# Retention and a gated feed-forward block in one kernel: other places for the sums of the second weight's quarters, and for the last steps of block 1

## The chip, the cores and the metric

The kernel runs on one core of a Trainium2 chip. The time is the device time of one execution in microseconds (us), and a kernel is judged by the median of several executions. TensorE (PE) multiplies matrices, VectorE (DVE), ScalarE (ACT) and GpSimd (POOL) work elementwise, SyncE (SP) only issues transfers (DMAs). Each engine takes its instructions in its own order, and semaphores hold an instruction until what it needs is there.

## The reference

Inputs are q, k, v of shape (4 batches, 8 heads, 768 positions, 64), w_in (512 x 2048) and w_out (2048 x 512), random, the weights in float64 on the way in (the kernel narrows them itself).

```python
gamma = 1.0 - 2.0 ** (-5.0 - np.arange(H))
for t in range(S):
    state = gamma * state + einsum('bhd,bhe->bhde', k[:, :, t], v[:, :, t])
    y[:, :, t] = einsum('bhd,bhde->bhe', q[:, :, t], state) / sqrt(D)
x = y.transpose(0, 2, 1, 3).reshape(3072, 512)
h = x @ w_in
out = (h / (1 + exp(-1.702 * h))) @ w_out
```

## The kernel before

**Chunks and steps.** The retention is computed in 24 chunks of 64 positions (two batches at once, 12 chunks per pair of batches). `turn(j)` transposes chunk j's q and k (from chunk 8 on by VectorE, L251) and issues the loads of q and k for chunk j+2 on SP (L154: 8 loads each). `step(j, f)` runs four groups of small matmuls on PE: the scores of chunk j (L287), the state's update (L295), and the output of the chunk before, f, from the state (L304) and from its own scores (L310). The first two write the PSUM tile `pa`, the others `py`; there is one buffer of each. Behind them VectorE masks the scores (L316), adds to the state (L366), and writes the output into the tile `X` (L328, L345). A step also issues the loads of k and v of the next chunk on SP (L140), and POOL decays k (`decay`, L272) and the state (`aged`, L357).

**Blocks.** Four chunks of two batches fill a block of 512 tokens; there are six blocks. Each block has a first product (x by w_in), the gating on ScalarE, and a second product (g by w_out). From block 2 on, the first product (`up`, L469) multiplies by Strassen and Winograd's scheme: seven products of halves in place of eight, with sums of the operands prepared beforehand. `sums_x` (POOL, L440 to L443) makes the sums of `X` in slots 2, 4, 5 and 6. The second product of blocks 0 and 1 (`down`, L705) has seven such products in 28 units (n = 0 to 27), each unit 4 matmuls, which the profile shows as 8 passes. Its sums of g (`sums_g`, DVE L456 to L458 and POOL L459) are made beside the third product (units 8 to 11), for the fourth (units 12 to 15). A kept sum behind unit 19 (DVE, L712) and the four output tiles (`put`: DVE L681, output DMA on POOL L682) follow the units that complete them; the last output follows unit 27. From block 2 on the second product (`down49`, L572) applies the scheme twice, and so needs sums of quarters of w_out.

**The sums of w_out's quarters.** For each of the seven outer products, `inner_w2(i)` derives three of them in `X` slots 4 to 6 (three subtractions on DVE, L519), and SP writes them to a DRAM tile `W2D[i]` (L520, 768 KB). All seven calls use the same place in `X`, so each call's first subtraction waits until the transfer before has landed, and `sums_x` of block 1, which writes the same slots, waits for the seventh. Slots 4 to 6 of `X` also hold a part of block 0's g, whose last reader in block 0's second product is unit 19. `inner_w2_t3(i)` makes a fourth sum in place (DVE, L525) once block 1's products have read that part of w_out.

**Order.** PE's instructions stand in the order of the text. For the other engines a scheduler of the compiler takes the calls in the order of the text as a wish and places each instruction by when its operands are expected to be there; only what is pinned keeps its order. In block 1 the steps stand between the units of the second product: `between` is a list of calls, and one is taken off after every third unit, half of them empty:

```python
between = [lambda: (decay(2 * CB), load(2 * CB + 1, "v"))]
for j in range(2 * CB + 1, 3 * CB + 1):
    between += [lambda j=j: (step(j, j - 1), j < 3 * CB and turn(j + 1)), lambda: None]
between.pop()
```

With CB = 4, that puts the steps of chunks 9, 10, 11 and 12 after units 5, 11, 17 and 23, and `sums_x` is called right behind the last.

Of the kernel before, what the change touches and what calls it, by code (L numbers as in the profile page):

```python
# [28 lines left out]
def kernel(  # L29
# [38 lines left out]
    CB = 4  # L68
# [55 lines left out]
    def load(j, what="qkv"):  # L124

        b, c = j // NC * 2, j % NC
        rows = slice(c * D, (c + 1) * D)
        keep = tc.keep_in_program_order if j < 2 * CB else lambda i: i  # L130

        def plain(name, src, tag, bufs, engine=sp):
            t = two.tile([P, H, D], F32, name=name + "_in", tag=tag, bufs=bufs)
            QKV[name, j] = t
            for i in range(2):
                if j < 2 * CB:
                    keep(engine.dma_start(t[i * D:(i + 1) * D], src[b + i, :, rows, :].rearrange("h p d -> p h d")))
                else:
                    for r in range(2):
                        keep(engine.dma_start(t[r * D:(r + 1) * D, i * HP:(i + 1) * HP],  # L140
                                              src[b + i, r * HP:(r + 1) * HP, rows, :].rearrange("h p d -> p h d")))

        if j < 2 * CB:
            if "q" in what:
                plain("q", q, "q_sq", 2)
            if "k" in what:
                plain("kn", k, "k_sq", 2, sp if j else act)
        elif "q" in what:
            for name, src in (("q", q), ("k", k)):
                t = two.tile([P, H, D // C4, C4], F32, name=name + "_sq")  # L150
                for r0 in range(0, P, C4):
                    for n in range(D // C4):
                        t0 = c * D + n * C4
                        tc.keep_in_program_order(sp.dma_start(  # L154
                            t[r0:r0 + C4, :, n], src[b + r0 // D, :, t0:t0 + C4, r0 % D:r0 % D + C4]
                            .rearrange("h p d -> p h d")))
                QKV[name, j] = t
        if "v" in what:
            if j >= 2 * CB and c < NC - 1:
                plain("kn", k, "kn", 1)  # L160
            plain("v", v, "v", 2)
# [66 lines left out]
    def home(j, name):  # L228

        at = ["qT", "kT", "kd", "at"].index(name)  # L230
        shape = [[HP, P] if j < 2 * CB else [H, D]] * 2 + [[H, D], [2, HP, D]]
        shape = shape[at]
        if j >= 2 * CB:
            return one.tile([P] + shape, F32, name=name, tag=name, bufs=[2, 1, 1, 2][at])
        t = G[:, at, j % 2 * 2:j % 2 * 2 + 2].rearrange("p s t -> p (s t)")
        return t.rearrange("p (a b c) -> p a b c", a=2, b=HP) if at == 3 else t.rearrange("p (a b) -> p a b", a=shape[0])

    def turn(j):

        QT[j], KT[j] = home(j, "qT"), home(j, "kT")  # L240
        if j < 2 * CB:

            x = QKV.pop(("q", j)), QKV["kn", j]
            TURNED[j] = p = [ps.tile([P, HP, P], F32, name="pt", tag="y") for i in range(2)]
            for n in (1, 0) if j else (0, 1):
                for s in range(HP):
                    for r in range(2):
                        pe.matmul(p[n][HALF[r], s, :], x[n][:, HP * r + s, :], ident, start=True, stop=True)  # L248
        else:
            for t, name in ((QT[j], "q"), (KT[j], "k")):  # L250
                tc.keep_in_program_order(dve.transpose(  # L251
                    t.rearrange("p h t -> p (h t)"), QKV.pop((name, j)).rearrange("p h n d -> p (h n d)")))
        if 2 * CB <= j < NCH - 2:
            load(j + 2, "qk")
# [6 lines left out]
    def decay(j):  # L261

        if j % NC == NC - 1:
            return
        KD[j] = home(j, "kd")
        x = QKV["kn", j]
        if j < 2 * CB:

            for h in range(H):
                pin(act.activation(KD[j][:, h], x[:, h], AF.Copy, scale=cold[:, H + h:H + h + 1]))  # L270
        else:
            pool.tensor_mul(KD[j].rearrange("p (i s) d -> p i s d", i=2), x.rearrange("p (i s) d -> p i s d", i=2),  # L272
                            cold[:, None, H:H + HP, None].to_broadcast([P, 2, HP, D]))
# [40 lines left out]
    def masked(j):  # L314
        AT[j] = home(j, "at")
        pin(dve.tensor_mul(AT[j], PA.pop(j)[:, :, 0],  # L316
                           mask if j < 2 * CB else mask[:, 0:1].to_broadcast([P, 2, HP, D])))
# [42 lines left out]
    def updated(f):  # L360
        c = f % NC
        new, u = state[(c + 1) % 2], PU.pop(f)
        if c == 0:
            pin(dve.tensor_copy(new, u))
        elif c < NC - 1:
            pin(dve.tensor_add(new, new, u))  # L366

    def step(j, f=None):
        attend(j, f)
        if j is not None:  # L370
            masked(j)
            if j > 2 * CB:
                decay(j)
        if f is not None:
            c = f % NC
            if c == 0:
                updated(f)
            else:
                by_state(f)
            output(f)  # L380
            if 0 < c < NC - 1:
                aged(f)
                updated(f)
        if j is not None and 2 * CB < j < NCH - 1:
            load(j + 1, "v")
# [123 lines left out]
    def w2q(w):  # L509

        return [W2[:, w, u::2, e * P:(e + 1) * P] for u in range(2) for e in range(2)]

    def inner_w2(i):

        b11, b12, b21, b22 = w2q(ORDER[i][1])
        t = []
        for k, a in enumerate((b12, b22, b21)):
            t.append(X[:, 4 + k].rearrange("p c (d e) -> p (c d) e", e=P))
            dve.tensor_sub(t[k], a, t[k - 1] if k else b11)  # L519
        sp.dma_start(W2D[i].rearrange("p k d e -> p (k d e)"), X[:, 4:7].rearrange("p k c t -> p (k c t)"))  # L520

    def inner_w2_t3(i):

        b11, b12, b21, b22 = w2q(ORDER[i][1])
        dve.tensor_sub(b12, b22, b12)  # L525
# [291 lines left out]
    for name, i in [("0a", 0), ("0b", 1)] + [(str(p), 2 * p) for p in range(1, NFF)]:  # L817
        n = Narrow(i)
# [20 lines left out]
    for name in """  # L839
# [16 lines left out]
    """.split():  # L856
        works[name]()
    ordered[0] = False
    for m in range(NB):
        between = []  # L860
        if m == 0:
            between = [lambda: turn(2 * CB), lambda: step(2 * CB), lambda: None, lambda: None, lambda: turn(2 * CB + 1)]
        elif m == 1:
            between = [lambda: (decay(2 * CB), load(2 * CB + 1, "v"))]
            for j in range(2 * CB + 1, 3 * CB + 1):
                between += [lambda j=j: (step(j, j - 1), j < 3 * CB and turn(j + 1)), lambda: None]
            between.pop()
        elif 1 < m < NB - 1:
            last = min((m + 2) * CB, NCH - 1)
            for j in range((m + 1) * CB + 1, last + 1):  # L870
                between.append(lambda j=j: (step(j, j - 1), j < last and turn(j + 1)))
            if last == NCH - 1:
                between.append(lambda: step(None, NCH - 1))
        if m > 1:
            if m > 2:
                W1B[:] = [late.tile([P, 2, 7, 2, P], F32, name=f"W1B{i}", tag=f"late{i}") for i in range(2)]
                pool.dma_start(W1B[0], W1D[0])
            for d in range(NP // 2):
                up(d)
                if d == 0 and m > 2:  # L880
                    pool.dma_start(W1B[1], W1D[1])
                if d == 0 and m < NB - 1:
                    turn((m + 1) * CB + 1)
                if d == NP // 2 - 2:
                    ring = begin_ring()
                if m == 2:
                    for i in range(2 * d, min(7, 2 * d + 2)):
                        inner_w2_t3(i)
        for n, unit in enumerate(down(m) if m < 2 else down49(m, *ring)):
            unit()  # L890
            if m == 0 and n < NP and n % 2:
                sums_w2(n - 1)
            if m == 0 and NP <= n < 3 * NP // 2:
                sums_w2_t3(2 * (n - NP))
            if m == 1 and n % 8 == 3:
                sums_w1(n // 4)
            if m == 1 and n % 3 == 1 and n < 21:
                inner_w2(n // 3)
            if between and (n % 3 == 2 if m < 2 else n % 3 == 1):
                between.pop(0)()  # L900
                if m == 1 and not between:
                    sums_x()
            if 1 < m < NB - 1 and n == 11:
                sums_x()
# [46 lines left out]
```

## Time and profile before

| | |
|---|---|
| median of 3 runs | 679.7 us (677.56 to 680.57) |
| the profiled execution | 678.85 us, its span on the core 676.7 us |
| PE busy | 655.5 us, 97% of the span |
| VectorE, POOL, ScalarE busy | 437.0, 170.4 and 156.9 us |
| granted clock of TensorE | 0.995 |
| block 0's second product on PE | 160.98 to 211.05 us of the span |
| block 1's second product, with its steps | 211.05 to 273.40 us |
| block 2's first product begins | 273.40 us |

The span runs from the first to the last instruction; the rest of the execution's time lies around it. A group of rows named "L705 PE MATMUL pd<-W,G" is line 705 on TensorE, which writes the tile pd from W and G. The time in brackets behind a row of the timeline is how long its engine sat idle before it, with what it waited for. SPq is the queue on which SP issues its transfers.

### The profile page before, as it was taken

How to read it: one execution, taken by the hardware profiler on the slowest of the kernel's cores; microseconds unless marked ns; L12 is line 12 of the kernel's file. 1: busy time of each engine (PE TensorE's matmuls, PEld its weight loads, DVE VectorE, ACT ScalarE, POOL GpSimd, SP SyncE). 2: the span in 40 equal slices, each digit the busy share in tenths (PEclk: the TensorE clock that was granted, in tenths of full speed). 3: DMA queues.
4: the chain of work that ended last, by engine and by line, in shares of the span. 5: the costliest groups of instructions: out<-in, count | busy, mean ns of one | idle time of the engine just before them, and what ended most of it. 6: DMA issues, size and time to landing. Idle time of an engine off the chain costs nothing.

```text
span 676.7 us, 15331 instructions
## 1 busy us (share of the span) xinstructions
PE 655.5 (97%) x6502; PEld 568.5 (84%) x6502; DVE 437.0 (65%) x614; ACT 156.9 (23%) x313; POOL 170.4 (25%) x189
## 2 busy tenths in 40 slices
PE   7799999999999979899999999999999999999997
PEld 4788864747888868688999988999988999988997
DVE  3688880879856686155887255898154896254865
ACT  5665523321000000133200133200133200133210
POOL 3000000020279151300245700245800244500000
PEclk9899999999999999899999999999999999999999
DMA  9999732332314835422177572178572153502142
GB/s 183 214 218 226 193 125 79 132 91 45 68 63 198 289 76 140 110 32 94 48 175 172 137 231 99 49 174 179 124 238 98 52 154 111 220 29 94 47 156 94
DMA packets 143780, 88.97 MB, mean 131 GB/s; under 512 B 129472, under 2 KB 130752, under 8 KB 142688
## 3 DMA queue, kind: packets, MB, share of 16 engines
q1 hardware_dynamic: 134656, 48.33, 31.0%
q0 software_dynamic: 6752, 38.42, 15.8%
q10 hardware_dynamic: 2304, 1.25, 0.6%
q8 instruction: 51, 0.84, 0.5%
q14 instruction: 17, 0.14, 0.1%
HBM read 72.37 MB, written 15.47 MB: 130 GB/s over the span
## 4 chain that ended last, share of the span: by engine, by line
PE 81%; DMA 7%; SPq 5%; DVE 5%; issue 1%; POOL 1%; ACT 0%; POOLq 0%
PE pq L572 26%; PE px L469 16%; PE py L469 12%; PE ph L425 8%; PE ph L412 8%; DMA W2D<-X 4%; SPq L154 4%; PE pd L705 3%; DVE X L519 3%; PE pt L248 2%; PE pa L295 1%; PE pa L287 1%; PE py L310 1%; DMA v_in<-in_v_dram 1%; PE py L304 1%; SPq L140 1%
## 5 line engine op out<-in xcount | busy, mean ns | idle before, releaser
L572 PE MATMUL pq<-W,G 128*128 128x128 f32 x672 | 80.3, 276 | 0.0
L572 PEld LDWEIGHTS pq<-W,G 128*128 128x128 f32 x672 | 77.6, 192 | 0.6
L541 POOL DMA_DIRECT2D ring<-W2D x28 | 15.4, 552 | 231.6 <-PE px L469 121.2
L469 PE MATMUL px<-X,W1A 128*128 128x256 f32 x256 | 61.3, 386 | 3.1 <-POOL X L442 3.1
L469 PE MATMUL px<-X,W1B 128*128 128x256 f32 x256 | 59.8, 379 | 0.0
L572 PE MATMUL pq<-ring,own 128*128 128x128 f32 x448 | 59.8, 276 | 0.0
L469 PEld LDWEIGHTS px<-X,W1A 128*128 128x128 f32 x256 | 49.0, 193 | 10.3 <-POOL X L442 3.5
L705 PE MATMUL pd<-W,G 128*128 128x256 f32 x224 | 50.4, 382 | 4.7 <-DVE G L458 4.7
L572 PEld LDWEIGHTS pq<-ring,own 128*128 128x128 f32 x448 | 54.5, 192 | 0.4
L469 PEld LDWEIGHTS px<-X,W1B 128*128 128x128 f32 x256 | 48.6, 190 | 6.6
L705 PEld LDWEIGHTS pd<-W,G 128*128 128x128 f32 x224 | 42.0, 190 | 11.7 <-DVE G L458 3.9
L469 PE MATMUL py<-X,W1A 128*128 128x256 f32 x192 | 45.8, 381 | 0.0
L469 PE MATMUL py<-X,W1B 128*128 128x256 f32 x192 | 45.4, 379 | 0.0
L391 ACT ACTIVATE G<-G 128x512 f32<-128x512 f32 x48 | 30.2, 630 | 52.0 <-DVE G L479 33.4
L469 PEld LDWEIGHTS py<-X,W1A 128*128 128x128 f32 x192 | 36.9, 192 | 5.2
L469 PEld LDWEIGHTS py<-X,W1B 128*128 128x128 f32 x192 | 36.5, 190 | 5.0
L487 DVE TENSOR_TENSOR t<-py,u 128x512 f32<-128x512 f32 x16 | 11.1, 691 | 40.5 <-PE py L469 40.5
L476 ACT ACTIVATE p<-px 128x512 f32<-128x512 f32 x16 | 9.6, 597 | 97.0 <-PE px L469 97.0
L412 PE MATMUL ph<-X,W1A 128*128 128x256 f32 x128 | 29.1, 383 | 0.5 <-DVE X L345 0.5
L572 PE MATMUL pq<-ring,G 128*128 128x128 f32 x224 | 29.6, 275 | 0.0
L572 PE MATMUL pq<-W,own 128*128 128x128 f32 x224 | 29.6, 275 | 0.0
L501 DVE TENSOR_TENSOR G<-G 128x512 f32<-128x512 f32 (+2 forms) x24 | 12.3, 513 | 25.7 <-ACT G L391 25.7
(202 smaller groups left out, 1178.5 us busy)
## 6 DMA issues: line engine op xcount, KB each, us to landing
ring<-W2D POOLq DMA_DIRECT2D x28, 768.0 KB, 4.9
W1B<-W1D POOLq DMA_DIRECT2D x6, 1792.0 KB, 9.1
W<-in_moe_w_in_dram SPq DMA_DIRECT2D x12, 512.0 KB, 6.5
W2D<-X SPq DMA_DIRECT2D x7, 768.0 KB, 3.7
W<-in_moe_w_out_dram SPq DMA_DIRECT2D x10, 512.0 KB, 4.4
out_dram<-o POOLq DMA_DIRECT2D x20, 256.0 KB, 3.5
v_in<-in_v_dram SPq DMA_DIRECT2D x64, 64.0 KB, 3.2
q_sq<-in_q_dram SPq DMA_DIRECT2D x128, 32.0 KB, 2.2
```

Of the source, the lines that this page charges most:

```text
L154: tc.keep_in_program_order(sp.dma_start(t[r0:r0 + C4, :, n], src[b + r0 // D, :, t0:t0 + C4, r0 % D:r0 % D + C4] .rearrange("h p d -> p h ...
L248: pe.matmul(p[n][HALF[r], s, :], x[n][:, HP * r + s, :], ident, start=True, stop=True)
L391: pin(act.activation(g, h[:, i], AF.Gelu_apprx_sigmoid))
L412: pe.matmul(h[:, ab], w, X[:, 2 * th + c // 2, c % 2, :], start=(ab == 0 and c == 0), stop=(c == 3), skip_group_check=True)
L425: pe.matmul(h, w, X1[:, c // 2:4:2, c % 2, :], start=(c == 0), stop=(c == 3))
L469: pe.matmul(acc[:, u, :], t[:, q1 + u, sa, c, :], X[:, sb, c, :], start=(start and u == 0 and c == 0), stop=(stop and c == 1), skip_group_ ...
L487: dve.tensor_add(tt, z, u)
L501: dve.tensor_sub(q[0][1], q[0][0], q[0][1])
L519: dve.tensor_sub(t[k], a, t[k - 1] if k else b11)
L541: pool.dma_start(c, W2D[i])
L572: pe.matmul(p0[:, j, :], a[:, d], w[:, d], start=(new and j == 0 and d == 0), stop=(d == NP // 2 - 1), skip_group_check=True)
L705: pe.matmul(p0[:, n, :], g1(m, p, sa)[:, n * P:(n + 1) * P], W2[:, sb, p, :], start=(new and p == 0 and n == 0), stop=(last and p == NP - ...
```

## The change

The seven calls of `inner_w2` get places by a list: in block 0 after units 19, 22 and 25 of the second product, in block 1 after units 0, 3, 13 and 17. Before, all seven were called in block 1, after units 1, 4, 7, 10, 13, 16 and 19. The empty calls in block 1's `between` are gone, and its entries are taken after units 2, 5, 11, 16 and 21: the step of chunk 11 comes after unit 16 (17 before), and that of chunk 12, with `sums_x` behind it, after unit 21 (23 before). The other blocks take their steps after the same units as before.

```diff
+    INNER = [(0, 19), (0, 22), (0, 25), (1, 0), (1, 3), (1, 13), (1, 17)]
     for m in range(NB):
...
             for j in range(2 * CB + 1, 3 * CB + 1):
-                between += [lambda j=j: (step(j, j - 1), j < 3 * CB and turn(j + 1)), lambda: None]
-            between.pop()
+                between.append(lambda j=j: (step(j, j - 1), j < 3 * CB and turn(j + 1)))
...
-            if m == 1 and n % 3 == 1 and n < 21:
-                inner_w2(n // 3)
-            if between and (n % 3 == 2 if m < 2 else n % 3 == 1):
+            if (m, n) in INNER:
+                inner_w2(INNER.index((m, n)))
+            if between and (n in (2, 5, 11, 16, 21) if m == 1 else n % 3 == (1 if m else 2)):
                 between.pop(0)()
                 if m == 1 and not between:
                     sums_x()
```

## The prediction, made before the changed kernel was run

> **What bounds the kernel now.** I read the page's busy shares first: TensorE (PE) is busy 97% of the span, so a change that adds and removes no matrix product can only win or lose in the stalls of PE. The waits of PE name the large ones (in the answer: engine and line, what it waited for, us in total, times, longest):
>
> ```profile
> PE 655.5 (97%) x6502; PEld 568.5 (84%) x6502; DVE 437.0 (65%) x614; ACT 156.9 (23%) x313; POOL 170.4 (25%) x189
> ...
> PE pd L705 <- DVE G L458: 4.7, 4, 2.0
> ...
> PE px L469 <- POOL X L442: 3.1, 1, 3.1
> ```
>
> Both lie in block 1's second product, the stretch that the diff edits: 7.8 us together, and nothing else there is to be won. Next I took the timeline of PE over that stretch (start us, us, what, idle before it and releaser):
>
> ```profile
> 246.87 5.45 PE L705 MATMUL pd<-W,G 128*128 128x256 f32 x24 [0.28 <-DVE G L458]
> 252.25 0.69 PE L287 MATMUL pa<-qT,kT 64*64 64x64 f32 x32
> ...
> 264.83 0.69 PE L287 MATMUL pa<-qT,kT 64*64 64x64 f32 x32
> ...
> 273.40 1.89 PE L469 MATMUL px<-X,W1A 128*128 128x256 f32 x8
> 275.12 1.89 PE L469 MATMUL py<-X,W1A 128*128 128x256 f32 x8
> 280.13 3.31 PE L469 MATMUL px<-X,W1A 128*128 128x256 f32 x8 [3.12 <-POOL X L442]
> ```
>
> The two L287 rows are the steps of chunks 11 and 12, the ones that the change moves; the stall of 3.12 us comes after both and after the 28th unit. The chain of waits says what that stall hangs on:
>
> ```profile
> 248.66 0.32 SPq L154
> ...
> 257.10 0.45 SPq L520
> ...
> 272.64 3.59 DMA W2D<-X
> 276.38 1.25 POOL X L440
> 277.63 1.22 POOL X L441
> 278.86 1.23 POOL X L442
> 280.13 2.03 PE px L469 x5
> ```
>
> So it is not a step of PE, but SP's queue: from 248.66 to 272.64 it issues without a pause of over 0.15 us (32 square loads of q and k, 8 loads of k and v, and one W2D at 257.10), then the last W2D, whose landing lets POOL start the sums of x. The queue starts at 248.66 because its first load waits for the transposes (L251) behind step 10:
>
> ```profile
> 246.74 0.68 DVE L316 TENSOR_TENSOR at<-pa,mask 128x512 f32<-128x512 f32 x1
> 247.34 0.67 DVE L366 TENSOR_TENSOR state<-state,pa 128x512 f32<-128x512 f32 x1
> 247.93 0.70 DVE L251 STREAM_TRANSPOSE qT<-q_sq 128x512 f32<-128x512 f32 x1
> ```
>
> These stand right behind the sums of g on VectorE (DVE), and ahead of anything that the change moves.
>
> **What the Trainium skill says.** "DMA: Bandwidth & Descriptors", section "Anatomy of one DMA", says that a semaphore wait is served on the issuing sequencer before dispatch, so a DMA that waits holds what is behind it. The trace agrees: the sixth W2D was computed by 236.0 (L519 at 235.32, 0.68) and left at 257.10. The same section fits a transfer at 2.0 us and bytes over 436e9 (for POOL's path); for 768 KB that estimate is 3.8 us, and the trace has 3.59 for the last W2D. "SBUF — State Buffer", section "SBUF: two separate sides", says that a VectorE operation with both inputs in SBUF is shut out while a GpSimd one reads SBUF: L457 took 0.69 us alone and 1.64 beside POOL's L459. I use the free value, 0.69, for the moved L519, since POOL is idle from 263.8 to 267.46.
>
> **The change, part by part.** PE's order is that of the text; for the other engines a scheduler places instructions, so I compared the built order of both programs.
>
> *1. Seven derivations (inner_w2) called earlier: 21 VectorE subtractions L519 and 7 SP DMAs L520.* Built, SP's and POOL's orders are the same instruction for instruction, and so is DVE's up to L712 of block 1 (258.10 in the trace). The scheduler had already put three sevenths in block 0: L519 starts at 192.26, 199.76 and 207.82, before block 1's first matmul at 211.05. So nothing is moved past anything: 0 us. In particular the 4.7 us before the sums of g stay. The same six L519 (0.68 to 0.71 each) still stand between 225.25 and 236.0, with the waits of 4.29 and 1.81 us for W2D transfers ahead of two of them. The new pattern of "between" gives block 0 and the later blocks the places they had: 0 us.
>
> *2. Step 11 on PE one unit earlier (after n=16, not 17), step 12 two units earlier (21, not 23).* A unit is 8 matmul passes: 273.40-266.39 = 7.01 us for four, 1.75 each. No work is added. Step 11 starts at about 252.25-1.75 = 250.50. It needs qT and kT (DVE done at 249.22, margin 1.3), kd (POOL done at 247.72; its first use is 0.5 later, margin 3.3) and PSUM "py" free of L345 of step 10 (done 250.52; the first L304 would come at 250.5+0.98 = 251.5, margin 1.0). So it doesn't wait. Step 12 follows at 264.83-2x1.75 = 261.3; its transposes, some 6 us earlier, and its v (issued by 246.14) are there. Cost 0. Unit 28 ends at 273.40 as before.
>
> *3. DVE's queue at 258 to 274.* In the built order step 12's L316 now stands ahead of the last three L519, and two L525 behind them. L316 holds the queue until PE's pa, about 261.3+0.7 = 262.0. Then L316, L519, L519, L328, L519 at 0.6 to 0.7 each, so the last L519 ends near 265.3, against 266.57 (265.88 and 0.69) now. That gain of 1.2 us is worth nothing: SP comes to the last W2D only at 272.64, 7.3 us later. The next L525 waits for the product that ends at n=23, now about 266.4; the two output sums L681 behind it go from 266.49 to about 267.1, and their output DMAs on POOL from 267.46 to 268.1. They landed in 2.7 to 4.3 us, and nobody waits for them before block 2.
>
> *4. Step 12's tail: sums_x after n=21.* Its first subtraction, L440, stands behind three output DMAs in POOL's queue, the third of which waits for the last unit:
>
> ```profile
> 274.59 0.73 POOL L682 DMA_DIRECT2D out_dram<-o  x1 [5.65 <-DVE o L681]
> 276.38 1.25 POOL L440 TENSOR_TENSOR X<-X 128x512 f32<-128x512 f32 x1 [1.06 <-DMA W2D<-X]
> ```
>
> So the sums cannot start before 275.32, even were the W2D there: at most 1.06 us could ever be had from placing step 12 earlier, and it needs an earlier SP. SP's loads behind step 11 wait for its transposes, which move from 255.97 to about 254.3, while SP reaches those loads at 263.63. No gain: 0.
>
> **Sum.** 0 + 0 + 0 + 0 us, against the profiled execution's own 678.85 us (span 676.7). The three timed runs are 677.56, 679.7 and 680.57; with the profiled one their median is (678.85+679.7)/2 = 679.3, which I take as the forecast. Their spread is 0.44%, so about 0.5% is what a measurement of this kernel can tell from no change.
>
> **Not shown by the trace, bounded.** (a) How the last W2D fares with the outputs' traffic 0.6 us nearer to it: the 7 transfers of its kind took 3.6 to 5.5 us, so from 0.0 to +1.9 for the last; I take 0, as the outputs still land by about 272.5. (b) A wait of PE at a step that comes earlier: it can cost no more than the work now behind it that used to be ahead, one unit for step 11 and two for step 12, 3.5 us; the stall of 3.12 us behind it takes up 1.06 before the third output delays L440, so 0 to +2.4; I take 0 for the margins above. (c) A gain in SP's chain: 0 to -1.06, by the third output; I take 0.
>
> **Rivals.**
> *A, nothing moves that anyone waits for* (as above): 679.3. Chance 0.91.
> *B, the change does what its text says*: the sums of g find DVE free and the sums of x come in time, 4.7+3.1 = 7.8 us, 671.5. For it: both stalls are there, and L519 with its W2D waits stands ahead of the sums of g. Against it: the built order leaves these instructions where they were. With the case that (c) and the spread of the runs come together, 0.05.
> *C, slower: step 12's L316 shuts DVE.* All three last L519, thus the last W2D, now hang on PE reaching step 12. It decides from the point where the third L519 ends after 272.64, that is if step 12 comes 7.3 us later than 261.3; each us more then delays L442 by one. At 11 us late, +3.7: 683.0. Against it: nothing on PE between step 11 and step 12 waits in the trace. With (a) and (b) coming together, +4.3, 683.6, as the other way to the same side: 0.04.
>
> **How the numbers follow.** Within 0.5%: 0.91 (A). Faster: 0.05 (B). Slower: 0.04 (C). The range is A's with (c) and noise below, 679.3-1.06-0.9 = 677.3, and (a) with about the same noise above, 681.3; 0.9 is a little over half the half-spread of the runs shown, for a median. It leaves out B and C.
>
> **What would show it.** Right: the timeline of PE has the steps at about 250.5 and 261.3, no new wait at L287 or L304, the waits of 4.7 (L458) and about 3.1 us (L442) unchanged, the last W2D issued near 272.6, and the first of block 2's held products near 280.1. Step 3 is right if L316 stands at about 262 with its L519 done by 265.5. Wrong: the wait for L442 gone or under 2 us, or the last W2D before 270 (then SP's chain depends on step 11 after all); or a wait of PE above 1 us at a step (then a margin of step 2 is wrong).

## The result, and the profile after

The changed kernel takes 679.46 us (median of 4 runs, 679.34 to 679.92), the kernel before 679.67 (median of 4, 677.56 to 680.57): a ratio of 1.0003, with a 95% interval of 0.9979 to 1.0026. No change can be told. The profiled execution took 679.92 us, its span 677.8.

The page's busy times and the waits of PE, after (engine, line, what it waited for; us in total, times, longest):

```profile
PE 656.3 (97%) x6502; PEld 568.8 (84%) x6502; DVE 437.9 (65%) x614; ACT 157.0 (23%) x313; POOL 169.9 (25%) x189
...
PE pd L705 <- DVE G L458: 3.4, 4, 2.1
PE px L469 <- POOL X L442: 2.9, 1, 2.9
```

The wait for the sums of g reads 3.4 us where it was 4.7. That is no gain, as the timeline of PE shows:

```profile
238.99 2.49 PE L705 MATMUL pd<-W,G 128*128 128x256 f32 x8 [2.08 <-DVE G L458]
241.90 2.87 PE L705 MATMUL pd<-W,G 128*128 128x256 f32 x8 [0.42 <-DVE G L458]
245.38 1.99 PE L705 MATMUL pd<-W,G 128*128 128x256 f32 x8 [0.61 <-DVE G L458]
247.65 3.72 PE L705 MATMUL pd<-W,G 128*128 128x256 f32 x16 [0.28 <-DVE G L458]
251.31 0.69 PE L287 MATMUL pa<-qT,kT 64*64 64x64 f32 x32
...
262.16 0.69 PE L287 MATMUL pa<-qT,kT 64*64 64x64 f32 x32
...
280.71 3.29 PE L469 MATMUL px<-X,W1A 128*128 128x256 f32 x8 [2.91 <-POOL X L442]
283.79 2.33 PE L469 MATMUL py<-X,W1A 128*128 128x256 f32 x8
285.96 1.89 PE L469 MATMUL px<-X,W1A 128*128 128x256 f32 x8
```

Before, the first three of these units stood like this (the fourth started at 246.87):

```profile
238.21 1.97 PE L705 MATMUL pd<-W,G 128*128 128x256 f32 x8 [2.02 <-DVE G L458]
241.11 1.99 PE L705 MATMUL pd<-W,G 128*128 128x256 f32 x8 [0.94 <-DVE G L458]
244.59 1.99 PE L705 MATMUL pd<-W,G 128*128 128x256 f32 x8 [1.48 <-DVE G L458]
```

Each of the four units behind the sums of g starts 0.78 or 0.79 us later than before, and 0.73 of that was there already where block 1 begins (211.78 against 211.05), in front of the first instruction that stands in another place. The first two units ran longer (2.49 and 2.87 us instead of 1.97 and 1.99) and so left less of the same gap: VectorE sets the starts, PE only fills them. What ran slower is the clock, in the stretch from 240 to 244 us of before and of after (stretch, length, PE busy, granted clock, DMA share, GB/s):

```profile
240.00:244.00 4.00, 2.17 (x9) 1.00 0.36 55
```
```profile
240.00:244.00 4.00, 3.58 (x11) 0.57 0.36 57
```

A wait that shrinks while the busy time grows is to be checked against the starts of the instructions.

The chain of waits, after, has the same end as before:

```profile
273.01 3.80 DMA W2D<-X
276.96 1.25 POOL X L440
278.21 1.23 POOL X L441
279.44 1.23 POOL X L442
```

### The profile page after: what moved, and what is told of

Same layout as the page of the kernel before. It is cut to its first block, busy times and chain, and to the rows that moved or that the text cites. A ratio compares the mean times of both kernels' runs of the same rounds, so it can differ in the third digit from the quotient of the medians.

```text
span 677.8 us, 15331 instructions
## 1 busy us (share of the span) xinstructions
PE 656.3 (97%) x6502; PEld 568.8 (84%) x6502; DVE 437.9 (65%) x614; ACT 157.0 (23%) x313; POOL 169.9 (25%) x189
## 4 chain that ended last, share of the span: by engine, by line
PE 90%; DVE 5%; DMA 3%; POOL 1%; SPq 1%; issue 1%; POOLq 0%
PE pq L572 26%; PE px L469 16%; PE py L469 12%; PE pd L705 11%; PE ph L425 8%; PE ph L412 8%; PE pt L248 2%; PE pa L287 2%; PE pa L295 2%; PE py L310 1%; PE py L304 1%; DMA v_in<-in_v_dram 1%; DMA kn_in<-in_k_dram 1%; DVE G L457 1%; DMA W2D<-X 1%
## 5 line engine op out<-in xcount | busy, mean ns | idle before, releaser
L469 PE MATMUL px<-X,W1A 128*128 128x256 f32 x256 | 61.2, 385 | 2.9 <-POOL X L442 2.9
L469 PE MATMUL px<-X,W1B 128*128 128x256 f32 x256 | 59.8, 379 | 0.0
L469 PEld LDWEIGHTS px<-X,W1A 128*128 128x128 f32 x256 | 48.9, 193 | 10.1 <-POOL X L442 3.3
L705 PE MATMUL pd<-W,G 128*128 128x256 f32 x224 | 51.8, 389 | 3.4 <-DVE G L458 3.4
L469 PEld LDWEIGHTS px<-X,W1B 128*128 128x128 f32 x256 | 48.6, 190 | 6.6
L705 PEld LDWEIGHTS pd<-W,G 128*128 128x128 f32 x224 | 42.8, 194 | 10.9 <-DVE G L458 2.8
L469 PE MATMUL py<-X,W1A 128*128 128x256 f32 x192 | 45.8, 382 | 0.0
L469 PE MATMUL py<-X,W1B 128*128 128x256 f32 x192 | 45.4, 379 | 0.0
L469 PEld LDWEIGHTS py<-X,W1A 128*128 128x128 f32 x192 | 36.9, 192 | 5.2
L469 PEld LDWEIGHTS py<-X,W1B 128*128 128x128 f32 x192 | 36.5, 190 | 5.0
```

The lines of the kernel that those rows point to most:

```text
L469: pe.matmul(acc[:, u, :], t[:, q1 + u, sa, c, :], X[:, sb, c, :], start=(start and u == 0 and c == 0), stop=(stop and c == 1), skip_group_ ...
L705: pe.matmul(p0[:, n, :], g1(m, p, sa)[:, n * P:(n + 1) * P], W2[:, sb, p, :], start=(new and p == 0 and n == 0), stop=(last and p == NP - ...
```

## The experiments

Ratios are to the kernel before, run beside each on the same chip. Diffs are to the changed kernel unless said otherwise. Where an edit adds a line near L456, later lines carry a number higher by one (L470 is L469, L520 is L519, L706 is L705). A product of block 2 here is one group of 8 passes at L469; there are seven to a set, and the third is the first that needs the sums of `X`. Theory: nothing that anyone waits for moved, and the two stalls are real and worth winning. Rivals: the stalls are hidden elsewhere and worth nothing; the change would have worked but for the scheduler's order.

**1. The calls at their new places, the steps left as before** (diff to before):

```diff
-            if m == 1 and n % 3 == 1 and n < 21:
-                inner_w2(n // 3)
+            if (m, n) in INNER:
+                inner_w2(INNER.index((m, n)))
```

> One part alone: the seven calls of inner_w2 at the new places, the steps where they were before (after units 5, 11, 17, 23). In the built order this keeps PE and DVE as before, but SP's queue has the last W2D ahead of the last v load and of the 16 loads of q and k behind step 11 (before: behind them), and POOL has the sums of x ahead of the third output DMA. Theory (the stall of 3.1 us at the start of block 2 hangs on SP's queue): the last W2D leaves at about 266.6, when its third L519 is done, lands near 270.2, L442 is done near 274.0, and PE, which wants it at 277.0, does not wait: 3.1 us faster than before, 676.3 against 679.4; the 4.7 us before the sums of g stay. Rival (the stall only moves: the loads behind the W2D come 3 us later and something in block 2 waits for them, or L442 waits for another thing): 679.4, with a new wait in block 2 or at L442.

Measured: 674.24 us, 0.9922 [0.9899, 0.9945]: half of the change is faster than the whole. The queue of SP and the timeline of POOL:

```profile
266.62 0.35 SPq L520 DMA_DIRECT2D W2D<-X  x1
...
268.21 4.58 SPq L154 DMA_DIRECT2D q_sq<-in_q_dram  x8
```
```profile
270.45 1.26 POOL L440 TENSOR_TENSOR X<-X 128x512 f32<-128x512 f32 x1 [1.49 <-DMA W2D<-X]
...
275.91 0.73 POOL L682 DMA_DIRECT2D out_dram<-o  x1
```

The last W2D leaves ahead of the loads of q and k (behind them, at 273.01, in the changed kernel), and the scheduler put the sums of `X` ahead of the third output's DMA. On PE and VectorE the order is that of the kernel before. PE, over the place of the stall:

```profile
275.14 1.89 PE L469 MATMUL py<-X,W1A 128*128 128x256 f32 x8
276.87 1.89 PE L469 MATMUL px<-X,W1A 128*128 128x256 f32 x8
278.60 1.89 PE L469 MATMUL py<-X,W1A 128*128 128x256 f32 x8
280.32 1.89 PE L469 MATMUL px<-X,W1A 128*128 128x256 f32 x8
```

No wait, and the products that took 3.31 and 2.31 us take 1.89. Before, the fourth and the fifth stood here:

```profile
283.23 2.31 PE L469 MATMUL py<-X,W1A 128*128 128x256 f32 x8
285.37 1.89 PE L469 MATMUL px<-X,W1A 128*128 128x256 f32 x8
```

The fifth product starts at 280.32 instead of 285.37: 5.05 us, of which 3.1 are the stall and (3.31-1.89)+(2.31-1.89) = 1.84 the slow passes behind it. So the stall is on the path, and dearer than its own length. The wait for the sums of g stayed (4.8 us).

The other half, the steps at their new places with the calls as before, has no run of its own: as built, its instructions stand on every engine in the order of the changed kernel. So the halves don't add up. With step 12 after unit 21, its L316 stands ahead of the last three L519 on VectorE, and the last W2D goes behind q and k on SP; that takes back what the calls bring.

**2. All W2D transfers from ScalarE's queue.**

```diff
-        sp.dma_start(W2D[i]...)
+        act.dma_start(W2D[i]...)
```

> The changed kernel with the W2D transfers issued by ScalarE (idle there) in place of SP. Theory (SP's queue holds them): W2D 5 leaves as soon as its L519 are done, near 236 (257 to 258 so far), the last one well before 262, L442 no longer holds PE (-2.9 us); in the built order two L519 of the last derivation now stand inside the sums of g on DVE, which costs up to 2 x 0.7 = 1.4 us there, so 1.5 to 3 us faster: 677.2. Rival (landing, not issue, is the limit): the last W2D still lands near 276, 679.5.

Measured: 680.1 us, 1.0006 [0.9988, 1.0023]. The gain that was expected did not come. The stall at L442 went, but as much came back elsewhere. Waits of PE, then VectorE's timeline:

```profile
PE pd L705 <- DVE G L458: 6.3, 3, 3.3
...
PE pa L287 <- DVE kT L251: 1.6, 1, 1.6
...
PE py L304 <- DVE X L345: 0.9, 1, 0.9
```
```profile
230.07 0.69 DVE L519 TENSOR_TENSOR X<-W 128x512 f32<-128x512 f32 x1 [10.18 <-DMA W2D<-X]
```

The corresponding L519 starts at 225.98 in the changed kernel. The W2D that it waits for took 10.7 us to land, the six others 3.2 to 3.8: freed from SP's queue, it left at 219.31, right behind both W1D transfers (L437, 1.8 MB each, issued at 215.42 and 218.76). In the changed kernel it stood between the two on SP and held the second back. The Trainium skill ("DMA: Bandwidth & Descriptors", section "Issuing engines are not separate DMA queues") says that transfers of all issuing engines end up on the same 16 DMA engines; the 10.7 us agree with that. That the W1D transfers are the cause is argued from their place; it wasn't isolated. Two L519 of the last derivation also stand between the sums of g here (at 243.44 and 245.25), as was expected; their part of the 6.3 us isn't separated either.

**3. L519 and the sums of g pinned in the order of the text.** In the changed kernel the scheduler draws derivations forward, so that all but the last stand ahead of the sums of g. Here only five can.

```diff
-        dve.tensor_add(a[3], a[2], a[3])
+        keep = tc.keep_in_program_order if m == 1 else lambda i: i
+        keep(dve.tensor_add(a[3], a[2], a[3]))     # the two subtractions alike
...
-            dve.tensor_sub(t[k], a, t[k - 1] if k else b11)
+            tc.keep_in_program_order(dve.tensor_sub(t[k], a, t[k - 1] if k else b11))
```

> The changed kernel with the L519 and block 1's L456 to L458 held in the order of the text, so that the scheduler can't lift the sixth derivation (called after unit 13) ahead of the sums of g, as it does in the kernels before and after. Theory: the sums of g start right behind the fifth derivation, near 232 in place of 236, PE's stall there falls from 4.7 to about 1 us; SP's chain to the last W2D, which starts with the transposes behind step 10, can follow only by about 2.5 us (its loads of q, k and v are issued without pause from 235 on), so the stall at L442 grows to some 4.5 us: 2.5 us faster in all, 677.0. Rival B of the prediction (the derivations are what holds the sums, and all of it comes back): 3.9 us faster, 675.5. Rival C' (the derivations moved behind the sums make the last W2D late): no gain, 679.5 or more.

Measured: 682.02 us, 1.0032 [1.002, 1.0044]: slower, where the theory had 677.0. The L519 of VectorE:

```profile
206.65 0.69 DVE L520 TENSOR_TENSOR X<-W 128x512 f32<-128x512 f32 x1 [4.89 <-DMA W2D<-X]
...
214.77 0.69 DVE L520 TENSOR_TENSOR X<-W 128x512 f32<-128x512 f32 x1 [2.53 <-DMA W2D<-X]
...
227.00 0.69 DVE L520 TENSOR_TENSOR X<-W 128x512 f32<-128x512 f32 x1 [6.51 <-DMA W2D<-X]
```

The first derivation now starts at 198.41, behind L712's sum that waits for a product, instead of 192.99 in the changed kernel. From there each derivation waits for the landing of the one before, and the fifth still ends in front of the sums of g, which begin at 237.84 (236.71 in the changed kernel). The waits at L458 and L442 are 5.9 and 3.9 us. So the sums of g are late for a chain of round trips (subtractions, transfer, landing: 7.7 to 12.2 us from one start to the next), not for the subtractions' own time (0.69 us each without a wait). And with these two kinds of instructions in the order of the text, the change does not win either, so the scheduler's order alone was not what kept it from working.

**4. Both: calls at their new places, steps as before, and the pins.**

> Both: the steps as before (5, 11, 17, 23), the calls of inner_w2 at the new places, and the L519 and block 1's L456 to L458 held in the order of the text. In the built order the last W2D stands ahead of the last v load and the loads of q and k of chunk 14. Theory (two separate stalls, one by the DVE order and one by SP's order): both go, 3.9 + 3.1 = 7.0 us, 672.4. Rival (they share a cause, so that the second gain is part of the first): 676.

Measured: 677.67 us, 0.9969 [0.9956, 0.9982]: neither of the two numbers expected. As in 1, the stall at L442 shrinks (0.7 us, the products behind it 1.99 and 1.89), and as in 3 the sums of g stay late (5.4 us), again with five round trips ahead of them.

**5. Only the last W2D from ScalarE's queue.**

```diff
-        sp.dma_start(W2D[i]...)
+        (sp if i < 6 else act).dma_start(W2D[i]...)
```

> The changed kernel with one thing different: the last W2D transfer is issued by ScalarE in place of SP. In the built order PE and DVE are as in the changed kernel; POOL's second and third output DMAs fall behind the sums of x. Theory (the place of the last W2D in SP's queue is the whole cause): it leaves right behind its third L519 near 267 (273.0 in the changed kernel), L442 is done before PE wants it at 277.6, so the stall of 2.9 us goes, and with it the slow passes right after it (3.29 and 2.33 us in place of 1.89 twice, granted clock 0.66 there): 2.9 + 1.8 = 4.7 us faster, 674.8. Rival 1 (the slow passes have another cause): 2.9 us, 676.6. Rival 2 (step (c) of the prediction, at most 1.06 us because of the third output): 678.4.

Measured: 673.36 us beside 679.44, 0.9911 [0.9892, 0.993]. ScalarE's queue, then POOL's and PE's timelines:

```profile
267.57 0.35 ACTq L520 DMA_DIRECT2D W2D<-X  x1
```
```profile
271.29 1.26 POOL L440 TENSOR_TENSOR X<-X 128x512 f32<-128x512 f32 x1 [0.29 <-DMA W2D<-X]
```
```profile
278.31 1.89 PE L469 MATMUL px<-X,W1A 128*128 128x256 f32 x8
```

The edit moves one issue from 273.01 to 267.57, past SP's 16 loads of q and k; the scheduler then also puts the DMAs of the second and third output behind L442 and L443 (in the changed kernel both came ahead of L440). From the first unit behind the sums of g to the fifth product of block 2 it is 281.77-239.67 = 42.10 us against 285.96-238.99 = 46.97: 4.87 us, the stall of 2.91 and slow passes of 1.84 again. That is the low end of the interval (-4.8 to -7.3 us); the other 1.2 us of the medians aren't accounted for. It shows that in the changed kernel the sums of `X` wait for SP's queue, as the prediction read the chain; how much of the gain would stay if the outputs kept their place, no run shows.

**6. PE kept busy in the stall.** Ahead of block 2's first held product PE runs three products of the identity with itself into a tile of `pa`; nothing reads them. No wait is taken away.

```diff
+            pe.matmul(..., ident, ident[:, None, :].to_broadcast([P, 4, P]), start=True, stop=True)   # three times
```

> The changed kernel with three matmuls of the identity into the idle PSUM tile pa, whose result nobody reads, put on PE in the place of the stall ahead of block 2's third product (each about 0.86 us, 2.6 us together; the stall is 2.9). Theory (PE's idle time lowers the granted clock, and the passes behind the stall pay for that): L442 still ends near 280.7, but the two products behind it take 1.73 us from start to start again in place of 3.1 and 2.2, so 1.8 us faster, 677.7. Rival (the passes are slow because of their operands or of POOL's L443 beside them): they stay slow, 679.5.

Measured: 676.62 us, 0.9961 [0.9948, 0.9973]. PE (L477 is L469 here, L467 the added products):

```profile
276.67 2.74 PE L467 MATMUL pa<-ident 128*128 128x512 f32 x6
279.83 1.99 PE L477 MATMUL px<-X,W1A 128*128 128x256 f32 x8 [0.42 <-POOL X L442]
281.66 1.89 PE L477 MATMUL py<-X,W1A 128*128 128x256 f32 x8
```

The third product still waits for L442, but from its start to that of the fifth it takes 3.55 us (283.38-279.83) instead of 5.25 (285.96-280.71): 1.70 of the 1.84 us. The operands are the same, and POOL's L443 runs beside it as before, so neither makes the passes slow. The interval of the ratio, -1.8 to -3.5 us, begins just above 1.70; the rest isn't accounted for. The stretch from 280 to 284, here and then in the changed kernel (the granted clock is the number behind the bracket):

```profile
280.00:284.00 4.00, 4.00 (x19) 1.00 0.02 6
```
```profile
280.00:284.00 4.00, 3.29 (x9) 0.66 0.11 23
```

The Trainium skill ("TensorE: Matmul & The Clock Gate", section "Part 1: The HAM clock gate") has it that an idle window of about 3.4 us halves PE's clock, that as long a busy one restores it, and that the window runs freely. This agrees in kind: the products take 1.89 us again from 285.96 on, 5.25 us behind the end of the stall. In length the trace is stricter: a stall of 2.91 us was enough.

**7. Four round trips ahead of the sums of g, and the late transfers off SP.** Steps as before, pins as in 3.

```diff
-    INNER = [(0, 19), (0, 22), (0, 25), (1, 0), (1, 3), (1, 13), (1, 17)]
+    INNER = [(0, 18), (0, 21), (0, 24), (1, 0), (1, 12), (1, 15), (1, 18)]
...
-        sp.dma_start(W2D[i]...)
+        (sp if i < 4 else act).dma_start(W2D[i]...)
```

> A version meant to lose both stalls: steps as before (5, 11, 17, 23), inner_w2 after units 18, 21 and 24 of block 0 and 0, 12, 15 and 18 of block 1, the L519 and block 1's L456 to L458 in the order of the text, so that four derivations and not six stand ahead of the sums of g; the first four W2D on SP, the last three on ScalarE. Theory: the sums of g begin as the third product's units end (near 229 in place of 236), the stall of 4.7 us goes, and so do the stall at L442 and its slow passes (3.1 + 1.8): 9.6 us faster than before, 670.0. Rival (as in the run where both parts were held in the order of the text, something else on DVE or in the W2D landings holds the sums): 674 or more.

Measured: 669.85 us beside 679.44, 0.9849 [0.9827, 0.9872], the fastest of all. VectorE, then PE:

```profile
227.43 0.69 DVE L457 TENSOR_TENSOR G<-G 128x512 f32<-128x512 f32 x1 [0.98 <-PE pd L706]
```
```profile
234.53 10.63 PE L706 MATMUL pd<-W,G 128*128 128x256 f32 x48
...
270.37 1.99 PE L470 MATMUL px<-X,W1A 128*128 128x256 f32 x8 [0.52 <-POOL X L442]
```

The sums of g now wait for PE, not for a landing, and PE runs 48 passes without a gap where the four waits were. From block 1's start to block 2's fifth product: 273.93-209.47 = 64.46 us against 285.37-211.05 = 74.32, 9.86 less. Of that, 4.7 is the wait at L458, 2.6 the one at L442 (3.1 to 0.5), 1.7 the slow passes. The other 0.8 lies in the six units behind the sums of g: 245.09-234.53 = 10.56 us to the next step, against 252.25-238.21 = 14.04 before, of which 2.7 were waits. A unit at whose end PE runs empty counts 1.97 or 1.99 us, where units in a row follow each other every 1.75. The edit changes several things together (the number of round trips, their start one unit earlier, the queue of the last three); which of them the gain at L458 needs was not run.

**8. The same with the changed kernel's steps** (after units 16 and 21):

> The version with four derivations ahead of the sums of g, now with the steps at the changed kernel's places (after units 16 and 21 in place of 17 and 23): the moved steps alone, where no stall hides them. In the built order POOL's sums of x now stand ahead of all three output DMAs. Theory (part 2 of the prediction: a step moved by one or two units neither adds work nor waits, margins of 1.0 us and more): the steps cost nothing, and the 0.5 us of waiting for L442 that was left goes: 669.4. Rival (a step now waits for DVE, which is busier here): a wait at L287 or L304, 670.5 or more.

Measured: 674.92 us beside 680.73, 0.9914 [0.9892, 0.9936]: (0.9914-0.9849) x 680 = 4.4 us of the 10.3 that experiment 7 won are lost. VectorE, then PE:

```profile
275.59 0.69 DVE L682 TENSOR_TENSOR o<-pd,t 128x512 f32<-128x512 f32 x1 [5.51 <-DMA out_dram<-o]
```
```profile
277.13 3.00 PE L470 MATMUL px<-X,W1A 128*128 128x256 f32 x8 [3.50 <-ACT p L477]
```

It is not mainly the steps that wait: L287 loses 0.2 us and L304 0.6. POOL now has `sums_x` ahead of all three output DMAs, which begin at 272.50; there are two tiles `o`, so the third output sum waits 5.51 us for one to land. ScalarE's copy `p` shares its place with `t`, which that sum reads, so it waits too, and PE waits 3.50 us to write the tile that is being copied. Neither expectation had this wait. The clock drops behind it once more (3.00 us for the third product).

## Why the prediction was right, point by point

- **What bounds the kernel** (PE; two stalls; the last hangs on SP's queue): right. Experiment 5 takes the issue off SP, and the stall goes. Only its place was misnamed: the stall at L442 stands in block 2, in its multiplication by w_in, not in block 1's second product. The rival that the stalls are worth nothing falls with experiments 1, 5 and 7.
- **Part 1, the calls move nothing: 0 us.** Right for the change as built: of the 0.78 us by which all four units shift, 0.73 come from the front. The sign that the wait of 4.7 us stays unchanged was not met as written (3.4 us), for the lower clock in between; the starts are what it was about. Experiment 1 bounds the 0: with the old steps the same calls are worth 5 us, so it belongs to the pair, not to the calls.
- **Part 2, the steps:** forecast 250.5 and 261.3 without a wait; 251.31 and 262.16 less 0.73 are 250.58 and 261.43, without a wait.
- **Part 3, VectorE's queue:** L316 forecast at 262.0, found at 262.92 (262.2 less the shift). The last L519 was to end at 265.3 and ended at 266.1 so reckoned. The term that failed is "POOL is idle from 263.8": POOL's L272 ran at 263.80, and one L519 beside it took 1.41 us instead of 0.69, the lock that the Trainium skill ("SBUF — State Buffer", section "SBUF: two separate sides") describes:

```profile
263.80 1.31 POOL L272 TENSOR_TENSOR kd<-kn_in,cold 128x512 f32<-128x512 f32 x1 [13.07 <-DMA kn_in<-in_k_dram]
```
```profile
264.25 1.41 DVE L519 TENSOR_TENSOR X<-W,X 128x512 f32<-128x512 f32 x1
```

The prediction could have seen it: before, L272 ran from 262.76 to 263.80, just where its own forecast put the first two of the L519. SP's lateness covers that, as forecast.

- **Part 4, the sums of `X`:** last W2D forecast near 272.6, found at 273.01; stall forecast 3.1, found 2.91. Right. The bound on a gain, "at most 1.06 us could ever be had", was right only with POOL's order of this build: in experiments 1 and 5 the scheduler put the sums ahead of an output, and the whole stall went.
- **"7.8 us together, and nothing else there is to be won"** was too small: it leaves out the passes at the lower clock behind the stall, 1.84 us by experiment 1 and 1.70 by experiment 6. Experiment 7 won 9.86 us in that stretch. Rival B's size was short by these 2 us; its rejection stands.
- **Rival C and the bounds (a), (b):** next to nothing showed. L316 did hold three L519, but SP came 6.1 us after the last of them (273.01-266.86). No step waited, and the last W2D took 3.80 us to land instead of 3.59, 0.2 of the 1.9 us allowed.
- **The range:** its upper end does not follow from its terms: 679.3+1.9+0.9 is 682.1, not 681.3. The measured time lies well inside either.
- The 1.07 us between the two profiled executions are 0.73 in front of block 1 and the rest behind it; with the interval of the ratio, no effect can be told from them.

## What to carry to other kernels

Read a change by the order that was built, not by the lines that moved: here one half of a change gave -5 us and the whole 0, since a call's place in the text is one thing, and what its instructions stand behind in each engine's queue another. When a stall hangs on a transfer, ask where in its queue the issue stands; moving one issue (experiment 5) brought 6 us, moving all seven nothing. A round trip through DRAM that reuses one buffer costs its landing, so count how many must fit ahead of the work that counts, rather than the time of their instructions.

## What was unexpected of the hardware

A stall of PE of about 3 us also slows what comes behind it: products of 1.89 us took 3.3 and 2.3 (mean clock from 280 to 284: 0.58 before, 0.66 after), 1.84 us on top of 3.1. Behind stalls of 0.4 to 0.7 us (experiments 4, 6 and 7) they took 1.99 and 1.89. Around the wait of 2 us for the sums of g the clock from 240 to 244 was 1.00 in the kernel before and in experiment 1, 0.57 in the changed kernel and in experiment 5 and 0.65 in experiment 6, with the same instructions ahead of it; that fits a window that runs freely, which no run here shows directly. There it cost nothing, since VectorE sets the starts.
